# Linear attention and a multiplicative FFN in one kernel: part of the casts and of phi's first instructions on GpSimd, in a new order of steps

## The chip, the core and the metric

The kernel runs on one core of a Trainium2 chip. The metric is the device time of one execution in microseconds (us), lower is better. A profile of one execution shows where that time goes; its span is the time from the first to the last event on the core, a little less than the device time.

## What is computed

```python
def phi(x):
    return np.where(x > 0, x, np.exp(x) - 1.0) + 1.0
# q, k, v: 8 batches, 8 heads, 576 positions, 64 columns, float32
q_p, k_p = phi(q), phi(k)
kv  = einsum('bhsd,bhse->bhde', k_p, v)
num = einsum('bhsd,bhde->bhse', q_p, kv)
den = einsum('bhsd,bhd->bhs', q_p, sum of k_p over s)[..., None] + 1e-06
x   = (num / den), as 4608 tokens by 512 columns
a, b = x @ w1, x @ w2              # w1, w2: 512 x 1024
out = ((a * b) @ w3) @ w_out       # w3: 1024 x 1024, w_out: 1024 x 512; out: 4608 x 512 float32
```

## The kernel before

**Algebra.** The kernel first multiplies w3 by w_out (the product is called Wf, 1024 x 512), so that the FFN is (a * b) @ Wf. All matmuls of the FFN and of Wf take bf16; inputs come from HBM as float32 and are cast.

**Steps and queues.** All work is cut into 490 steps, and the string ORDER lists them. The last lines of the kernel go through ORDER and call one small function per step (s_T3 for T3 and so on). Nothing reorders them afterwards: each engine and each DMA queue works off its instructions in the order of the string, and waits where an operand isn't there or a buffer isn't free. So ORDER sets the order on TensorE (PE), VectorE (DVE), ScalarE (ACT), GpSimd (POOL) and on SyncE's DMA queue (SP), which issues nearly all DMAs. A last letter a, v or p names the engine of a step that can be done by several: ACT, DVE or POOL.

The steps, with the letters of their indices:

- **Loads** (SP, 512 or 576 KB each, into one of 13 buffers): L3.i is block i of w3 (8 blocks; block 0 comes as two halves, LH.0.0 and LH.0.1), LO.x a quarter of w_out, LA.x and LB.x quarters of w1 and w2 (6 and 7 hold columns 0 to 511, 2 and 3 the rest), LQ.b.h, LK.b.h, LV.b.h half of the heads of batch b.
- **Casts**: CO.x, CA.x, CB.x cast such a quarter to bf16 (128 x 1024, lines 207, 211, 216), C3.i a block of w3 (line 227), VC.b.h a half of v (128 x 1152, line 285).
- **Wf**: T3.i.x transposes half of block i of w3 on PE (four 128 x 128 transposes, line 241) and copies the result to SBUF (line 242); FW.i.x does two of the eight matmuls of row block i of Wf (line 253), and needs CO.x; after the last (x = 3) Wf's block is cast to SBUF (line 255).
- **phi**: phi(x) is computed as min(max(x, 0) + 1, exp(x)). PT.n.b.h (n is q or k) does the max and the add in one instruction from float32 to bf16 (line 275, on DVE), EX.n.b.h the exponential on ACT (line 263), and PM.n.b.h the min on DVE (line 282).
- **Attention**: KV and KB build k_p^T v (line 298; KV half a batch in two 64-row tiles, KB a whole batch), QP transposes phi(q) on PE (line 326) and QD does it by DMA instead (line 331); ND (one tile of 128 tokens) and NT with NM (three tiles) form numerator and denominator on PE (line 344) and divide on DVE (line 350). KV, KB, ND and NT use PE in tiles of 64 x 64.
- **x transposed**: XP on PE (line 403, copy on line 404), XD by DMA transpose (line 408).
- **FFN**: chunks c0 of 512 tokens, 9 of them. F.c0.f is block f of 8: four matmuls for a, four for b (line 428, 128 x 512 each), a copied from PSUM by ACT (line 437), and a * b on DVE (line 439). FI does one of the two sides of an F, FP half the tokens of a side, for chunk 0 while the weights arrive. O.t multiplies token tile t by Wf (8 matmuls, line 463) and copies the result out of PSUM (line 470). Q.35 is the last tile, in pieces. S.t stores a tile (two DMAs of 128 KB).

PSUM holds four banks for FFN and Wf ("mm") and two double banks for the rest ("at"). Each F takes two of the four banks, so the second F after one needs its banks again.

**Start.** Nothing of chunk 0 can start before w3, w_out, w1, w2 and batch 0 have passed the DMA queue, 13 loads at a time, so for the first 45 us PE works on what has arrived: w3's transposes and Wf, then batch 0, then chunk 0.

What the change touches is ORDER and s_PT (line 273); copy_of (line 123) already gives GpSimd's copy for the letter p. The prediction's steps are in s_CO, s_CA, s_CB, s_VC, s_EX, s_PM, s_F and s_FI.

Of the kernel before, what the change touches and what calls it, by code (L numbers as in the profile page):

```python
# [18 lines left out]


ORDER = """
L3.2 I.0 LO.0 I.1 T3.2.0.a CO.0.v FW.2.0.a T3.2.1.a LO.1 CO.1.a L3.4 T3.4.0.v T3.4.1.v H.1 L3.3
T3.3.0.a LO.2 FW.4.0.v FW.4.1.a LO.3 L3.5 T3.3.1.v C3.5.a CO.2.v FW.2.1.a FW.2.2.a CO.3.v FW.2.3.v
L3.6 C3.6.v FW.3.0.a FW.3.1.v LK.0.0 T3.5.0.v LH.0.0 T3.5.1.v LQ.0.0 FW.4.2.v EX.k.0.0 PT.k.0.0
FW.4.3.a EX.q.0.0 T3.6.0.v PM.k.0.0 FW.5.0.v FW.5.1.v L3.1 T3.6.1.a PT.q.0.0 PM.q.0.0 L3.7 FW.5.2.v
FW.6.0.a FW.3.2.a FW.3.3.v FW.5.3.v LQ.0.1 T3.1.0.a C3.7.v T3.1.1.a FW.1.0.v FW.1.1.a LK.0.1
PT.q.0.1 EX.q.0.1 PM.q.0.1 T3.7.0.a FW.6.1.v FW.6.2.a FW.6.3.a LV.0.0 I.2 T3.0.0.v LV.0.1 EX.k.0.1
PT.k.0.1 T3.7.1.a LH.0.1 FW.7.0.a FW.7.1.v FW.1.2.v VC.0.0.v QP.0.0.v QP.0.1.a FW.7.2.a KV.0.0.a
PM.k.0.1 VC.0.1.v FW.7.3.v FW.1.3.a KV.0.1.v T3.0.1.a ND.0 FW.0.0.v LA.6 ND.1 FW.0.1.v CA.6.a LA.7
CA.7.a ND.2 FW.0.2.a XP.0.a XP.1.a ND.3 FW.0.3.a FP.0.0.0.0 LB.6 LQ.1.1 EX.q.1.1 LB.7 LA.3 XP.2.v  # L30
XP.3.v FP.0.1.0.0 CB.7.a LA.2 FP.0.1.0.1 LB.3 PT.q.1.1 PM.q.1.1 FI.0.2.0 FI.0.3.0 CB.6.v FI.0.1.1
LB.2 CA.2.a LQ.1.0 CB.3.v FP.0.0.0.1 FI.0.0.1 FI.0.3.1 CB.2.v QP.1.1.v CA.3.a PT.q.1.0 LK.1.0
FI.0.2.1 PT.k.1.0 EX.q.1.0 PM.q.1.0 F.0.4 EX.k.1.0 PM.k.1.0 F.0.5 LV.1.0 VC.1.0.a F.0.6 LK.1.1
EX.k.1.1 PT.k.1.1 PM.k.1.1 LV.1.1 LK.3.0 KV.1.0.a VC.1.1.a F.0.7 LQ.3.1 QP.1.0.a KV.1.1.v PT.k.3.0
EX.q.3.1 EX.k.3.0 O.0.a LQ.3.0 EX.q.3.0 PT.q.3.1 ND.4 ND.5 O.1.a XP.4.a ND.6 ND.7 PM.k.3.0 LK.2.0
XP.5.a O.2.a PM.q.3.1 XP.6.v XP.7.v LQ.2.1 EX.k.2.0 LQ.2.0 PT.k.2.0 PM.k.2.0 PT.q.3.0 EX.q.2.0
LK.3.1 PM.q.3.0 O.3.a LV.4.1 F.1.0 LV.2.0 LK.4.1 S.0.s F.1.1 PT.q.2.1 EX.q.2.1 S.1.s PT.k.3.1 F.1.2
EX.k.3.1 PM.k.3.1 LK.2.1 PM.q.2.1 F.1.3 VC.2.0.a LV.2.1 PT.k.2.1 PT.q.2.0 PM.q.2.0 EX.k.2.1 F.1.4
LV.3.0 F.1.5 VC.2.1.a PM.k.2.1 F.1.6 LV.3.1 VC.3.0.v QD.2.1 EX.k.4.1 KB.2.a QD.2.0 VC.3.1.a ND.8
QD.3.0 F.1.7 KB.3.a NT.9 NM.9.0 NM.9.1 QD.3.1 XD.2.0 NM.9.2 XD.2.1 S.2.s LK.4.0 O.4.v O.5.v NT.12  # L40
LV.4.0 NM.12.0 O.6.v NM.12.1 O.7.v NM.12.2 LQ.4.1 PT.k.4.0 F.2.0 F.2.1 F.2.2 F.2.3 F.2.4 EX.k.4.0
PT.k.4.1 LQ.5.1 F.2.5 PM.k.4.1 F.2.6 VC.4.0.a LQ.4.0 VC.4.1.a PM.k.4.0 F.2.7 S.3.s S.4.s LQ.5.0
LK.5.1 PT.q.5.0 EX.q.5.0 NT.15 PM.q.5.0 EX.q.4.1 NM.15.0 PT.q.4.1 PM.q.4.1 PT.q.4.0 LQ.7.1 S.5.s
KB.4.a PT.k.5.1 O.8.v EX.k.5.1 S.6.s LK.5.0 EX.k.5.0 PT.k.5.0 XD.3.0 XD.3.1 O.9.a O.10.a O.11.v
LV.5.1 F.3.0 PM.k.5.1 LK.6.0 F.3.1 PM.k.5.0 EX.q.4.0 NM.15.1 NM.15.2 LV.5.0 S.7.s S.8.s LK.6.1 F.3.2
S.9.s S.10.s VC.5.0.v PM.q.4.0 QD.4.0 EX.k.6.0 QD.4.1 F.3.3 F.3.4 EX.q.5.1 PT.q.5.1 PM.q.5.1
PT.k.6.1 F.3.5 F.3.6 F.3.7 QD.5.1 O.12.v NT.18 QD.5.0 NM.18.0 XD.4.0 NM.18.1 VC.5.1.a PT.k.6.0
KB.5.a XD.4.1 LQ.6.1 O.13.a O.14.v PT.q.7.1 O.15.v F.4.0 EX.q.7.1 PM.q.7.1 F.4.1 F.4.2 NM.18.2
LK.7.0 F.4.3 NT.21 EX.k.6.1 NM.21.0 NM.21.1 NM.21.2 LV.6.0 VC.6.0.v F.4.4 F.4.5 S.11.s S.12.s
PT.k.7.0 LK.7.1 LQ.7.0 F.4.6 LV.6.1 VC.6.1.v S.13.s S.14.s F.4.7 PT.q.7.0 PM.k.6.1 LQ.6.0 PM.k.6.0  # L50
O.16.v EX.q.7.0 O.17.v PM.q.7.0 PT.q.6.1 LV.7.0 O.18.v XD.5.0 XD.5.1 EX.q.6.1 PM.q.6.1 LV.7.1
VC.7.0.a S.15.s EX.q.6.0 KB.6.a NT.24 O.19.v NM.24.0 PT.q.6.0 PM.q.6.0 QD.6.1 F.5.0 VC.7.1.v
EX.k.7.1 PT.k.7.1 F.5.1 F.5.2 EX.k.7.0 NM.24.1 NM.24.2 QD.7.1 PM.k.7.0 F.5.3 F.5.4 QD.6.0 PM.k.7.1
F.5.5 S.16.s S.17.s NT.27 XD.6.0 NM.27.0 NM.27.1 QD.7.0 KB.7.a NM.27.2 F.5.6 XD.6.1 XD.7.0 F.5.7
S.18.s NT.30 S.19.s O.20.v S.20.s F.6.0 NM.30.0 NM.30.1 NM.30.2 F.6.1 XD.7.1 O.21.v NT.33 O.22.v
NM.33.0 NM.33.1 O.23.v F.6.2 F.6.3 F.6.4 F.6.5 F.6.6 F.6.7 F.7.0 F.7.1 F.7.2 F.7.3 F.7.4 F.7.5 F.7.6
S.21.s S.22.s S.23.s XD.8.0 NM.33.2 XD.8.1 O.24.a O.25.v O.26.v O.27.v S.24.s S.25.s S.26.s S.27.s
F.7.7 F.8.0 F.8.1 F.8.2 F.8.3 F.8.4 F.8.5 F.8.6 F.8.7 O.28.a O.29.a O.30.a S.28.s S.29.s S.30.s
O.31.v S.31.s O.32.v S.32.s O.33.v S.33.s O.34.a S.34.b Q.35
"""  # L60


# [1 line left out]
def kernel(  # L64
# [202 lines left out]
    def by_set(n, t):  # L267

        if n == "k":
            return t.rearrange("p (c j d) -> p c j d", c=2, j=J)  # L270
        return t.rearrange("p (j c d) -> p c j d", c=2, j=J)

    def s_PT(n, b, h, e):
        t = phs[n, b, h] = take("ph" + n, None, [P, HW], BF16, "ph" + n)
        nc.vector.tensor_scalar(out=by_set(n, t), in0=by_set("k", raw[n, b, h]), scalar1=0.0, scalar2=1.0,  # L275
                                op0=ALU.max, op1=ALU.add)
# [254 lines left out]
```

## Time and profile before

| | us |
|---|---|
| median of 3 runs | 243.22 |
| lowest, highest | 242.29, 243.37 |
| the profiled execution | 241.6 |
| its span | 239.8 |
| PE busy in it | 227.6 |
| DVE busy | 157.9 |
| ACT busy | 113.9 |
| POOL busy | 1.3 |

The profile gives, per engine, the busy time and groups of equal instructions with the mean duration of one in nanoseconds; the chain of waits goes back from the last instruction to what released each step. In a row of the timeline the first number is the start and the second the duration, both in us, "x4" counts the instructions merged into the row, and brackets hold the idle time before it and what ended it. PE's matmuls overlap each other, so a row of them is longer than the time that it adds; the chain gives what it adds.

### The profile page before, as it was taken

To read this page: it belongs to the slowest core of one execution; us is meant where nothing else is said; L and a number is where in the kernel's file an instruction comes from. 1 tells how busy PE (TensorE), PEld (TensorE's weight loads), DVE (VectorE), ACT (ScalarE), POOL (GpSimd) and SP (SyncE) were. 2 spreads that over 40 slices of the span, in tenths; PEclk is the share of its full clock that TensorE was granted. 3 is DMA by queue.
4 is the path that set the end of the run, shared out by engine and by line. 5 is a ranking of instruction groups with operands and counts; after the bars stand their busy time and mean duration, and the time that the engine had idled before them with its cause. 6 is when DMAs were issued, how large, how long until landed. Compare 5 with 4: busy or idle time off the path is not lost.

```text
span 239.8 us, 5452 instructions
## 1 busy us (share of the span) xinstructions
PE 227.6 (95%) x2218; PEld 114.4 (48%) x2237; DVE 157.9 (66%) x287; ACT 113.9 (48%) x166; POOL 1.3 (1%) x9
## 2 busy tenths in 40 slices
...
GB/s 247 420 382 403 387 386 389 389 392 389 400 278 129 160 347 392 340 190 358 233 108 271 385 362 177 169 202 112 137 121 78 3 0 44 164 13 0 46 155 148
DMA packets 52041, 55.79 MB, mean 233 GB/s; under 512 B 31281, under 2 KB 31537, under 8 KB 52017
## 3 DMA queue, kind: packets, MB, share of 16 engines
...
q8 instruction: 17, 0.28, 0.5%
q10 hardware_dynamic: 240, 0.26, 0.3%
...
## 4 chain that ended last, share of the span: by engine, by line
PE 92%; DMA 3%; issue 2%; DVE 1%; SPq 1%; ACT 0%; DVEq 0%
PE b_ps L428 26%; PE o_ps L463 26%; PE a_ps L428 26%; PE wf_ps L253 5%; PE nd L344 3%; DMA w<-in_moe_w_dram 3%; PE w3p L241 2%; PE kbp L298 2%; PE qp L326 1%; PE xp L403 1%; PE kvp L298 1%; SPq L155 1%; DVE xt L404 0%; DVE ab L439 0%; DVE w3t L242 0%
## 5 line engine op out<-in xcount | busy, mean ns | idle before, releaser
L428 PEld LDWEIGHTS <-w_sb 128*128 128x128 bf16 x584 | 56.5, 98 | 67.2 <-issue 1.4
L437 ACT COPY a_sb<-a_ps 128x512 f32<-128x512 f32 x72 | 42.2, 587 | 80.4 <-PE a_ps L428 78.5
L439 DVE TENSOR_TENSOR ab<-a_sb,b_ps 128x512 bf16<-128x512 f32 x72 | 49.0, 685 | 38.2 <-PE b_ps L428 36.4
L428 PE MATMUL a_ps<-xt,w_sb 128*128 128x512 bf16 (+1 forms) x296 | 74.0, 373 | 0.1
L428 PE MATMUL b_ps<-xt,w_sb 128*128 128x512 bf16 x288 | 73.8, 379 | 0.1
L463 PE MATMUL o_ps<-wf_sb,ab 128*128 128x512 bf16 (+2 forms) x290 | 63.5, 368 | 1.2 <-issue 0.6
L463 PEld LDWEIGHTS <-ab 128*128 128x128 bf16 x304 | 28.3, 98 | 31.2
L470 DVE COPY o_sb<-o_ps 128x512 f32<-128x512 f32 x23 | 15.8, 689 | 20.7 <-PE o_ps L463 18.9
L350 DVE TENSOR_TENSOR xn<-nd,r 128x512 bf16<-128x512 f32 (+2 forms) x45 | 24.2, 577 | 0.5
L263 ACT ACTIVATE eq<-q 128x1152 bf16<-128x1152 f32 x16 | 18.4, 1164 | 4.8 <-DVE phk L282 3.1
L263 ACT ACTIVATE ek<-k 128x1152 bf16<-128x1152 f32 x16 | 18.7, 1167 | 2.6 <-DMA k<-in_k_dram 2.6
L253 PE MATMUL wf_ps<-wo_sb,w3t 128*128 128x512 bf16 x59 | 16.0, 387 | 2.6 <-DVE wo_sb L207 1.8
L470 ACT COPY o_sb<-o_ps 128x512 f32<-128x512 f32 x12 | 6.9, 581 | 15.0 <-PE o_ps L463 15.0
L275 DVE TENSOR_SCALAR phk<-k 128x1152 bf16<-128x1152 f32 x16 | 12.0, 752 | 1.3 <-DMA k<-in_k_dram 1.3
L282 DVE TENSOR_TENSOR phq<-phq,eq 128x1152 bf16<-128x1152 bf16 x16 | 12.0, 751 | 1.2 <-ACT eq L263 0.5
L241 PE MATMUL w3p<-ident,w 128*128 128x128 f32 x40 | 8.2, 352 | 4.8 <-DMA w<-in_moe_w_dram 4.8
L282 DVE TENSOR_TENSOR phk<-phk,ek 128x1152 bf16<-128x1152 bf16 x16 | 11.9, 751 | 0.2
L275 DVE TENSOR_SCALAR phq<-q 128x1152 bf16<-128x1152 f32 x16 | 12.0, 752 | 0.0
L285 ACT CAST vt<-v 128x1152 bf16<-128x1152 f32 x9 | 10.3, 1160 | 0.0
L241 PEld LDWEIGHTS w3p<-ident,w 128*128 128x128 f32 x40 | 7.0, 214 | 6.4 <-issue 4.7
L253 PEld LDWEIGHTS <-w3t 128*128 128x128 bf16 x64 | 5.6, 98 | 7.1 <-issue 1.5
L344 PEld LDWEIGHTS <-qt 64*64 64x64 bf16 x576 | 6.2, 106 | 4.6 <-issue 3.0
...
## 6 DMA issues: line engine op xcount, KB each, us to landing
k<-in_k_dram SPq DMA_DIRECT2D x16, 576.0 KB, 9.0
q<-in_q_dram SPq DMA_DIRECT2D x16, 576.0 KB, 9.3
v<-in_v_dram SPq DMA_DIRECT2D x16, 576.0 KB, 7.9
...
w<-in_moe_w_dram SPq DMA_DIRECT2D x7, 512.0 KB, 9.5
wo<-in_moe_w_out_dram SPq DMA_DIRECT2D x4, 512.0 KB, 6.7
wa<-in_moe_w_dram SPq DMA_DIRECT2D x4, 512.0 KB, 11.5
wb<-in_moe_w_dram SPq DMA_DIRECT2D x4, 512.0 KB, 11.4
```

Source lines behind the costliest of these rows:

```text
L241: nc.tensor.transpose(tp[:, c, :], blocks[:, 2 * x + c // 2, c % 2, :], idt)
L253: nc.tensor.matmul(wfs[i], w3ts[i][:, c, :], wo_sb[:, c, :], start=(c == 0), stop=(c == FC - 1))
L263: nc.scalar.activation(out=t, in_=raw[n, b, h], func=AF.Exp)
L275: nc.vector.tensor_scalar(out=by_set(n, t), in0=by_set("k", raw[n, b, h]), scalar1=0.0, scalar2=1.0, op0=ALU.max, op1=ALU.add)
L282: nc.vector.tensor_tensor(out=t, in0=t, in1=by_set("k", es[n, b, h]), op=ALU.min)
L344: nc.tensor.matmul(dst[g * R:(g + 1) * R], qts[b, a // 2][rows, j, a % 2 * R:(a % 2 + 1) * R], kvs[b][rows, a // 2, a % 2, :], start=True, ...
L350: nc.vector.tensor_tensor(out=xn[:, :, a0:a1], in0=n4[:, :, :, 0:D], in1=r.unsqueeze(3).to_broadcast([P, 2, a1 - a0, D]), op=ALU.mult)
L428: nc.tensor.matmul(ops_[key][:, tiles.start * P:tiles.stop * P], w[:, w_row(kc), f * P:(f + 1) * P], xts[c0][:, tiles, kc, :], start=(kc = ...
L437: nc.scalar.copy(out=a_sbs[c0, f], in_=ops_[key])
L439: nc.vector.tensor_mul(out=abs_[c0][:, f, :], in0=a_sbs[c0, f], in1=ops_[key])
L463: nc.tensor.matmul(o_ps, abs_[c0][:, f, m * P:(m + 1) * P], wf_sb[:, f, cols], start=(f == 0), stop=(f == FC - 1))
L470: copy_of(e)(out=o_sbs[t], in_=o_ps)
```

## The change

ORDER is a new one, with the same 490 steps. Letters differ: 34 steps carry p, so they run on POOL, which had none but a few small ones before.

| steps | before | after |
|---|---|---|
| PT (32) | 32 DVE | 13 DVE, 19 POOL |
| VC (16) | 9 ACT, 7 DVE | 5 ACT, 4 DVE, 7 POOL |
| CO (4) | 1 ACT, 3 DVE | 1 DVE, 3 POOL |
| CA, CB (8) | 5 ACT, 3 DVE | 2 ACT, 1 DVE, 5 POOL |
| O (35) | 12 ACT, 23 DVE | 25 ACT, 10 DVE |

Smaller moves between ACT and DVE: T3 (9 ACT and 7 DVE before, 6 and 10 after), XP (4 and 4, then 7 and 1), QP (2 and 2, then 4 and 0), KB (6 and 0, then 4 and 2), KV (2 and 2, then 3 and 1). The loads come in another order: q.0.1 is 5th instead of 15th, w_out's second to fourth quarters are 6th to 8th instead of 3rd, 6th and 7th, the halves of w3's block 0 are 18th and 21st instead of 11th and 19th, and q.1.1 is 32nd, behind all weights, instead of 23rd. Which w3 blocks are cast to bf16 first (5, 6, 7), and which transposes run on PE and which by DMA, is as before.

```diff
@@ s_PT
-        nc.vector.tensor_scalar(out=by_set(n, t), in0=by_set("k", raw[n, b, h]), scalar1=0.0, scalar2=1.0,
-                                op0=ALU.max, op1=ALU.add)
+        (nc.gpsimd if e == "p" else nc.vector).tensor_scalar(
+            out=by_set(n, t), in0=by_set("k", raw[n, b, h]), scalar1=0.0, scalar2=1.0,
+            op0=ALU.max, op1=ALU.add)
@@ ORDER, up to the end of chunk 1, and the tail
-L3.2 I.0 LO.0 I.1 T3.2.0.a CO.0.v FW.2.0.a T3.2.1.a LO.1 CO.1.a L3.4 T3.4.0.v T3.4.1.v H.1 L3.3
-T3.3.0.a LO.2 FW.4.0.v FW.4.1.a LO.3 L3.5 T3.3.1.v C3.5.a CO.2.v FW.2.1.a FW.2.2.a CO.3.v FW.2.3.v
-L3.6 C3.6.v FW.3.0.a FW.3.1.v LK.0.0 T3.5.0.v LH.0.0 T3.5.1.v LQ.0.0 FW.4.2.v EX.k.0.0 PT.k.0.0
-FW.4.3.a EX.q.0.0 T3.6.0.v PM.k.0.0 FW.5.0.v FW.5.1.v L3.1 T3.6.1.a PT.q.0.0 PM.q.0.0 L3.7 FW.5.2.v
-FW.6.0.a FW.3.2.a FW.3.3.v FW.5.3.v LQ.0.1 T3.1.0.a C3.7.v T3.1.1.a FW.1.0.v FW.1.1.a LK.0.1
-PT.q.0.1 EX.q.0.1 PM.q.0.1 T3.7.0.a FW.6.1.v FW.6.2.a FW.6.3.a LV.0.0 I.2 T3.0.0.v LV.0.1 EX.k.0.1
-PT.k.0.1 T3.7.1.a LH.0.1 FW.7.0.a FW.7.1.v FW.1.2.v VC.0.0.v QP.0.0.v QP.0.1.a FW.7.2.a KV.0.0.a
-PM.k.0.1 VC.0.1.v FW.7.3.v FW.1.3.a KV.0.1.v T3.0.1.a ND.0 FW.0.0.v LA.6 ND.1 FW.0.1.v CA.6.a LA.7
-CA.7.a ND.2 FW.0.2.a XP.0.a XP.1.a ND.3 FW.0.3.a FP.0.0.0.0 LB.6 LQ.1.1 EX.q.1.1 LB.7 LA.3 XP.2.v
-XP.3.v FP.0.1.0.0 CB.7.a LA.2 FP.0.1.0.1 LB.3 PT.q.1.1 PM.q.1.1 FI.0.2.0 FI.0.3.0 CB.6.v FI.0.1.1
-LB.2 CA.2.a LQ.1.0 CB.3.v FP.0.0.0.1 FI.0.0.1 FI.0.3.1 CB.2.v QP.1.1.v CA.3.a PT.q.1.0 LK.1.0
-FI.0.2.1 PT.k.1.0 EX.q.1.0 PM.q.1.0 F.0.4 EX.k.1.0 PM.k.1.0 F.0.5 LV.1.0 VC.1.0.a F.0.6 LK.1.1
-EX.k.1.1 PT.k.1.1 PM.k.1.1 LV.1.1 LK.3.0 KV.1.0.a VC.1.1.a F.0.7 LQ.3.1 QP.1.0.a KV.1.1.v PT.k.3.0
-EX.q.3.1 EX.k.3.0 O.0.a LQ.3.0 EX.q.3.0 PT.q.3.1 ND.4 ND.5 O.1.a XP.4.a ND.6 ND.7 PM.k.3.0 LK.2.0
-XP.5.a O.2.a PM.q.3.1 XP.6.v XP.7.v LQ.2.1 EX.k.2.0 LQ.2.0 PT.k.2.0 PM.k.2.0 PT.q.3.0 EX.q.2.0
-LK.3.1 PM.q.3.0 O.3.a LV.4.1 F.1.0 LV.2.0 LK.4.1 S.0.s F.1.1 PT.q.2.1 EX.q.2.1 S.1.s PT.k.3.1 F.1.2
-EX.k.3.1 PM.k.3.1 LK.2.1 PM.q.2.1 F.1.3 VC.2.0.a LV.2.1 PT.k.2.1 PT.q.2.0 PM.q.2.0 EX.k.2.1 F.1.4
-LV.3.0 F.1.5 VC.2.1.a PM.k.2.1 F.1.6 LV.3.1 VC.3.0.v QD.2.1 EX.k.4.1 KB.2.a QD.2.0 VC.3.1.a ND.8
-QD.3.0 F.1.7 KB.3.a NT.9 NM.9.0 NM.9.1 QD.3.1 XD.2.0 NM.9.2 XD.2.1 S.2.s LK.4.0 O.4.v O.5.v NT.12
...
-NM.33.0 NM.33.1 O.23.v F.6.2 F.6.3 F.6.4 F.6.5 F.6.6 F.6.7 F.7.0 F.7.1 F.7.2 F.7.3 F.7.4 F.7.5 F.7.6
-S.21.s S.22.s S.23.s XD.8.0 NM.33.2 XD.8.1 O.24.a O.25.v O.26.v O.27.v S.24.s S.25.s S.26.s S.27.s
-F.7.7 F.8.0 F.8.1 F.8.2 F.8.3 F.8.4 F.8.5 F.8.6 F.8.7 O.28.a O.29.a O.30.a S.28.s S.29.s S.30.s
-O.31.v S.31.s O.32.v S.32.s O.33.v S.33.s O.34.a S.34.b Q.35
+L3.1 LO.0 L3.5 I.0 I.1 T3.1.0.v T3.1.1.v C3.5.v T3.5.0.v L3.2 T3.2.0.a LQ.0.1 LO.1 PT.q.0.1.v H.1
+CO.0.p LO.3 FW.5.0.v LO.2 L3.7 FW.2.0.v CO.1.p L3.4 L3.3 T3.5.1.v CO.3.p FW.1.0.a LQ.0.0 PT.q.0.0.p
+EX.q.0.1 PM.q.0.1 I.2 L3.6 LK.0.0 LV.0.0 VC.0.0.p LK.0.1 LV.0.1 LH.0.0 T3.2.1.a CO.2.v LA.7 LA.6
+C3.7.v FW.2.1.a QP.0.1.a LH.0.1 FW.1.1.v FW.1.2.a FW.1.3.a LB.6 LB.7 FW.5.1.v FW.5.2.a CA.6.p LA.2
+EX.q.0.0 FW.5.3.v T3.7.0.v FW.2.2.a FW.2.3.v T3.4.0.v LA.3 FW.7.0.a T3.7.1.v C3.6.a PT.k.0.0.v
+T3.4.1.a T3.3.0.a LQ.1.0 FW.4.0.a FW.4.1.v EX.k.0.0 CB.6.p LB.3 LB.2 FW.7.1.a FW.7.2.a FW.7.3.a
+T3.3.1.v PM.k.0.0 LK.1.0 CB.7.p FW.4.2.v FW.4.3.a T3.6.0.a PM.q.0.0 CA.2.p LK.1.1 FW.3.0.v EX.k.0.1
+T3.6.1.v PT.q.1.0.p FW.3.1.v FW.3.2.v QP.0.0.a CB.2.p KV.0.0.a FW.6.0.a FW.6.1.v FW.6.2.a PT.k.1.0.p
+PT.k.0.1.v PM.k.0.1 LV.1.0 VC.0.1.v KV.0.1.a T3.0.0.a ND.0 FW.3.3.a ND.1 LQ.1.1 CA.7.a FW.0.0.v
+FW.0.1.a ND.2 XP.0.a XP.1.a ND.3 FW.6.3.a T3.0.1.v XP.2.a FP.0.0.0.0 FP.0.1.0.0 XP.3.v FW.0.2.a
+FW.0.3.a FP.0.0.0.1 LV.1.1 FI.0.3.0 FI.0.3.1 EX.q.1.0 FI.0.0.1 PM.q.1.0 LV.2.0 FP.0.1.0.1 FI.0.1.1
+CA.3.a FI.0.2.0 CB.3.v FI.0.2.1 EX.k.1.0 LK.2.1 F.0.4 LK.3.0 QP.1.0.a VC.1.0.v PM.k.1.0 PT.k.1.1.p
+F.0.5 LQ.2.1 EX.k.1.1 PM.k.1.1 PT.q.1.1.p F.0.6 EX.q.1.1 PM.q.1.1 KV.1.0.a VC.1.1.a F.0.7 QP.1.1.a
+KV.1.1.v LQ.3.1 O.0.a LQ.2.0 LK.2.0 ND.4 ND.5 O.1.a XP.4.a PT.q.3.1.p LV.3.0 ND.6 PT.k.2.1.p ND.7
+PT.q.2.0.v EX.k.2.1 LK.3.1 XP.5.a O.2.a PT.k.3.0.p LV.2.1 LQ.4.0 LV.3.1 XP.6.a XP.7.a VC.2.0.p
+LQ.3.0 EX.q.2.0 PT.k.2.0.v PM.k.2.1 EX.k.2.0 PM.k.2.0 O.3.a S.0.s PT.q.2.1.v F.1.0 S.1.s PM.q.2.0
+VC.2.1.p QD.2.0 PT.q.3.0.p F.1.1 EX.k.3.0 PM.k.3.0 F.1.2 PT.k.3.1.p EX.q.3.1 EX.k.3.1 F.1.3 F.1.4
+PM.q.3.1 ND.8 VC.3.0.a EX.q.2.1 KB.2.a EX.q.3.0 PM.q.2.1 QD.2.1 PM.q.3.0 QD.3.0 F.1.5 F.1.6 PM.k.3.1
+F.1.7 QD.3.1 VC.3.1.p KB.3.a NT.9 NM.9.0 NM.9.1 XD.2.0 O.4.a O.5.a NM.9.2 XD.2.1 S.2.s NT.12 NM.12.0
+LK.5.0 LQ.5.0 LK.4.0 S.3.s O.6.a PT.k.4.0.p O.7.a F.2.0 PT.k.5.0.v S.4.s F.2.1 NM.12.1 NM.12.2
...
+PM.q.7.1 NM.27.1 O.20.v O.21.v QD.7.0 O.22.a F.6.0 F.6.1 S.18.s S.19.s S.20.s S.21.s F.6.2 F.6.3
+F.6.4 F.6.5 NM.27.2 S.22.s O.23.a QD.7.1 NT.30 NM.30.0 S.23.s NM.30.1 XD.7.0 NM.30.2 F.6.6 F.6.7
+O.24.v O.25.a O.26.a XD.7.1 F.7.0 F.7.1 F.7.2 O.27.v S.24.s NT.33 NM.33.0 S.25.s S.26.s XD.8.0
+NM.33.1 NM.33.2 F.7.3 F.7.4 F.7.5 XD.8.1 S.27.s F.7.6 F.7.7 F.8.0 F.8.1 F.8.2 O.28.v O.29.a O.30.a
+F.8.3 F.8.4 F.8.5 S.28.s S.29.s S.30.s O.31.a F.8.6 F.8.7 S.31.s O.32.a S.32.s O.33.a S.33.s O.34.a
+S.34.b Q.35
```

28 lines of the change are left out of this document (13 added, 15 removed).

## Prediction

> **What bounds the kernel now.** First the page: the span, each engine's busy share, the chain that ended last, and the sizes of loads.
>
> ```profile
> span 239.8 us, 5452 instructions
> ...
> PE 227.6 (95%) x2218; PEld 114.4 (48%) x2237; DVE 157.9 (66%) x287; ACT 113.9 (48%) x166; POOL 1.3 (1%) x9
> ...
> PE 92%; DMA 3%; issue 2%; DVE 1%; SPq 1%; ACT 0%; DVEq 0%
> ...
> k<-in_k_dram SPq DMA_DIRECT2D x16, 576.0 KB, 9.0
> ...
> wo<-in_moe_w_out_dram SPq DMA_DIRECT2D x4, 512.0 KB, 6.7
> ```
>
> PE is the chain for 92% of the span. Next the list of who waits for whom, the stages (columns: PE, PEld, DVE, ACT, POOL busy, granted clock, DMA share, GB/s), and the chain within the long middle stage.
>
> ```profile
> DVE ab L439 <- PE b_ps L428: 36.4, 42, 1.3
> ```
>
> ```profile
> 14.43:34.66 20.23, 19.36 (x253) 11.64 (x258) 17.14 (x34) 13.79 (x20) 0.00 (x0) 1.00 1.05 390
> 34.66:44.70 10.04, 9.94 (x66) 5.56 (x66) 8.50 (x15) 8.09 (x11) 0.00 (x0) 1.00 1.05 386
> ...
> 60.44:222.80 162.36, 161.41 (x1575) 76.36 (x1585) 110.82 (x199) 70.39 (x108) 0.00 (x0) 1.00 0.74 190
> ```
>
> ```profile
> by line: PE b_ps L428 34.1%; PE a_ps L428 33.8%; PE o_ps L463 25.6%; PE nd L344 2.8%; PE kbp L298 2.5%; issue 0.7%; DVE ab L439 0.4%; DVEq L439 0.0%
> ```
>
> In its commonest instruction DVE waits for PE, 36.4 us in all, not PE for DVE. From 60.44 to 222.80 only issue and DVE are not PE in the chain: 0.7% and 0.4% of 162.36 us, 1.8 us. So relief of DVE or ACT is worth at most that there, whatever its size. From 14.43 to 44.70 the DMA share is 1.05: the loads run without a break, and they set when work becomes possible. What PE loses at the start shows in the chain up to 60 us (start, duration, what):
>
> ```profile
> 2.14 6.33 DMA w<-in_moe_w_dram
> ...
> 12.59 0.48 PE w3p L241 x4
> ...
> 13.09 0.69 DVE w3t L242
> 13.78 0.61 DVE wo_sb L207
> ...
> 17.80 0.22 PE w3p L241 x4
> 18.02 0.86 PE wf_ps L253 x4
> ...
> 20.26 1.56 issue
> 21.81 0.59 ACT w3t L242
> ...
> 31.70 0.25 PE nd L344 x16
> ...
> 35.26 0.24 PE xp L403 x4
> ...
> 35.52 0.85 DVE xt L404 x2
> ...
> 43.13 0.86 PE a_ps L428 x4
> ...
> 50.56 0.50 PE qp L326 x9
> 51.06 0.41 PE kvp L298 x36
> 51.48 0.16 issue
> ```
>
> Four losses: 6.33 us until the second w3 block (PE works for part of that on the first), 1.3 us at 13.09 and 13.78 (w3t, then w_out's cast on DVE), 2.2 us at 20.26 and 21.81, 0.85 us at 35.52 (xt's copies). So at most 1.3 + 2.2 + 0.85 = 4.4 us could be won by an order of the start, if the loads allowed it. The other rows give what a step adds to the chain: a T3 0.48 (0.22 in bf16), an FW 0.43, an ND 0.25, an XP 0.24, half an F 0.86, a QP 0.50, a KV 0.41.
>
> **The change part by part.**
>
> *GpSimd's price.* POOL's trace ends after 2 us with these rows; the durations on the other engines stand beside them.
>
> ```profile
> L138 POOL CAST ident<-ident 128x128 bf16<-128x128 f32 x1 | 0.3, 289 | 0.1
> masks.py:197 POOL MEMSET ident<- 128x128 f32 x1 | 0.2, 204 | 0.3 <-POOLq L515 0.3
> L515 POOL MEMSET const-bfloat16-1.0<- 128x1 bf16 x1 | 0.1, 101 | 0.0
> ```
>
> ```profile
> L439 DVE TENSOR_TENSOR ab<-a_sb,b_ps 128x512 bf16<-128x512 f32 x72 | 49.0, 685 | 38.2 <-PE b_ps L428 36.4 <-ACT a_sb L437 1.5
> ...
> L263 ACT ACTIVATE eq<-q 128x1152 bf16<-128x1152 f32 x16 | 18.4, 1164 | 4.8 <-DVE phk L282 3.1 <-DMA q<-in_q_dram 1.7
> ...
> L275 DVE TENSOR_SCALAR phq<-q 128x1152 bf16<-128x1152 f32 x16 | 12.0, 752 | 0.0
> ...
> L282 DVE TENSOR_TENSOR phq<-phq,eq 128x1152 bf16<-128x1152 bf16 x16 | 12.0, 751 | 1.2 <-ACT eq L263 0.5
> ...
> L285 ACT CAST vt<-v 128x1152 bf16<-128x1152 f32 x9 | 10.3, 1160 | 0.0
> ...
> L285 DVE CAST vt<-v 128x1152 bf16<-128x1152 f32 x7 | 5.3, 756 | 0.0
> ...
> L207 DVE CAST wo_sb<-wo 128x1024 bf16<-128x1024 f32 x3 | 2.0, 687 | 4.3 <-DMA wo<-in_moe_w_out_dram 4.3
> ```
>
> A cast of 128 columns takes 289 ns, a memset of one column 101: (289 - 101) / 127 = 1.48 ns a column, so an estimate of 1.61 us for 1024 columns and 1.80 us for 1152. I take these, since the cast is the only row that reads and converts as the new ones do. Low end, by the memset of 128 columns: (204 - 101) / 127 = 0.81 ns, 0.93 and 1.04 us. High end, the cast's row without a fixed part: 8 x 0.289 = 2.31 and 9 x 0.289 = 2.60 us. DVE does the same in 0.69 and 0.75 us, ACT a v in 1.16. The Trainium skill, GPSIMD Engine Reference, § Performance versus the Vector engine, speaks against the move: for elementwise work it calls GpSimd structurally slower, but gives 1.03 to 1.8 cycles an element at 1.2 GHz for light loops, 0.99 to 1.73 us for 1152; by that the sum would be at its better end.
>
> *Load on the engines.* POOL gets 8 x 1.61 + 26 x 1.80 = 59.7 us (34.5 to 86.1), DVE loses 19 x 0.752 = 14.3 us for PT alone. None of it is on PE's chain: worth 0 by itself. What counts is when each result is there, below.
>
> *The start.* The loads are the clock of this stage. Two rows fix their pace:
>
> ```profile
> 4.24 1.10 PE L241 MATMUL w3p<-ident,w 128*128 128x128 f32 x4 [4.24 <-DMA w<-in_moe_w_dram]
> ...
> 31.63 0.21 PEld L344 LDWEIGHTS <-qt 64*64 64x64 bf16 x16 [0.42 <-issue]
> ```
>
> ```profile
> 43.23 1.16 ACT L263 ACTIVATE eq<-q 128x1152 bf16<-128x1152 f32 x1 [1.49 <-DMA q<-in_q_dram]
> ```
>
> The first 512 KB are there at 4.24; q.1.0, the 29th load, at 43.23, after 19 units of 512 KB (halves joined) and 8 of 576: 14,336 KB in 38.99 us, 1.39 us per 512 KB and 1.57 per 576. By this pace the new order has w_out's 2nd quarter at 11.4, its 4th at 12.8 and 3rd at 14.2, v.0.1 at 27.6, LB.7 at 34.5, LB.2 at 41.7, k.1.0 at 43.2, q.1.1 at 47.9, v.1.1 at 49.5. In PE's order:
>
> - CO.1 on POOL is done at 11.4 + 1.61 = 13.0, so FW.2.1 starts there; CO.2 stays on DVE: 14.2 + 0.69 = 14.9, FW.1.2 ends at 15.4 (CO.3 on POOL, 14.6, is in time).
> - From there to F.0.4 PE has 26 FW (11.2 us), 6 T3 in float32 (2.9) and 4 in bf16 (0.9), QP.0.0, 2 KV (1.3), 4 ND (1.0), 4 XP (1.0), 4 FP at 0.43 (1.7) and 6 FI (5.2): 25.2 us, 40.6 without a wait. I add 1.3 us for three waits: KV.0.1 for v.0.1 and its cast (28.4), ND's two banks, T3.0.1 and x's copies behind them. F.0.4 begins at 41.9.
> - Before, F.0.4 is the row at 43.13, with QP.1.1 (0.50) already done: like for like 42.6. So 0.7 us are won so far.
> - F.0.4's b side, at 41.9 + 0.86 = 42.8, needs CB.2 on POOL: 41.7 + 1.61 = 43.3. The win shrinks by 0.5 us; F.0.4 ends at 44.2.
> - QP.1.0, F.0.5 to F.0.7 and KV.1.0 take 6.1 us, to 50.3. QP.1.1 needs q.1.1 through PT on POOL and PM: 47.9 + 1.80 + 0.75 = 50.5. KV.1.1 ends at 51.4; before, the chain passes that point at 51.48.
>
> So the start is worth -0.1, call it 0. With POOL's low prices CB.2 and PT.q.1.1 come in time and it is -0.9; with the high ones +0.7.
>
> *PM behind POOL.* DVE works in order: where a PM waits for its PT on POOL, the a * b of the F's behind it (685 ns) waits too, and PE stops when an F's bank isn't free for the second F after it. Worst is q.3.0, the last load of its group, 13 loads after v.1.1: 49.5 + 13 x 1.57 = 69.9. F.1.0 at 60.44 as before, five F (8.65), ND.8 and KB.2 (0.25 and, as an estimate, two KV, 0.82) put F.1.5 at 70.2, the end of its matmuls at 71.9 and of its product at 72.6. PT is done at 71.7 and PM at 72.5, so the product ends at 73.1. F.1.7's b needs that bank at 70.2 + 2 x 1.73 + 0.86 = 74.5. Cover 1.4 us, cost 0; with 2.60 us for PT the product ends at 73.9, still 0. Buffers of loads that POOL frees later: 13 of them, and a load is issued some 9 us ahead (page's last column) of the 18 us that 13 loads take, so 0.
>
> *64 x 64 groups.* PE turns to 64 x 64 tiles 21 times instead of 20; the timeline's row at 31.63 shows 0.42 us of idle weight loading at such a turn. +0.3 (0 to 0.42).
>
> *The end.* F.8.7 now stands directly ahead of O.32, whose first seven matmuls (7 x 0.216) cover its product; the last tile is stored as before: 0. O on ACT instead of DVE: both wait for PE: 0.
>
> **Sum:** 0 + 0.3 on the profiled execution, 241.6 (span 239.8 and 1.8 around it), gives 241.9. That execution lies 1.6 below the median of 243.22, so the prediction for the median is 243.5, with 242.3 to 244.4 from the bounds above. A measurement of this kernel tells about 0.5% (1.2 us) from no change.
>
> **The rivals.**
>
> 1. *The start wins.* The three waits don't happen, POOL costs its low price and the loads keep up: F.0.4 at 40.6 against 42.6, minus 2.0; some of the 1.8 us of the middle stage may go too. With the 0.3 for the turns: 241.5, at best 239.7. It needs LB.2 at 40.5 or so instead of 41.7, a pace of 1.35 us per 512 KB. For it: 4.4 us of losses in the chain. Against: LB.2 is the 28th load in both orders, and the DMA share is 1.05.
> 2. *POOL and DVE hold each other up* while both work from SBUF: a PM, PT or cast on DVE waits until a running POOL instruction ends. At the start PM.q.0.1 (due 11.4: q.0.1 at 10.0, EX of 1.16 us behind a copy on ACT) stands behind CO.1 to 13.0, then CO.3 behind PM, CO.2 behind CO.3: FW.1.2 comes at 16.1 instead of 15.0, +1.1. Later, 29 POOL instructions (51 us) lie between LA.6's landing (31.1) and the middle of chunk 5 (60.44, four chunks and their O at 12 x 1.73, half a chunk: some 150), four tenths of the time. So of some 40 PM and PT on DVE there 16 wait half a POOL instruction, 0.9 us, 14 us in all. Where delays add up beyond the cover of 1.4 us PE stops; with a fifth felt, +3. Sum 243.2 + 1.1 + 3 + 0.3 = 247.6. It decides from the point where one wait and the instruction's own 0.75 us outlast the cover. No row bears on it, as POOL is idle after 2 us. The Trainium skill, SBUF — State Buffer, § Who interferes with whom, says this: DVE in a 2-port mode, or with two SBUF inputs, and GpSimd lock each other out of a shared port pair for a whole instruction; by it, this rival's time.
> 3. *POOL's two-operation PT is dearer* than any row bounds, say 4 us: CB.2's place is kept, but PT.q.1.1 is done at 51.9 and QP.1.1 waits to 52.7: +2.2; and F.1.5's product ends at 75.3, 0.8 late: in sum 243.2 + 2.2 + 0.8 + 0.3 = 246.5. POOL's load would be 117 us, still no bound.
>
> **How the numbers follow.** Forecast 0.38; the start wins 0.26; hold-up 0.22; dear PT 0.14. Range 240.8 to 247.6: it reaches to the rivals on both sides and leaves out a start that wins more and a hold-up felt more. Faster by over 0.5%: rival 1 and a little of the forecast's low end, 0.28. Slower by over 0.5%: rivals 2 and 3, 0.36. Within: 0.36.
>
> **What would show it.** POOL casts of 1.6 and PT of 1.8 us; KV.1.1's end near 51.4; no PE gap from F.1.5 to F.1.7; 21 turns to 64 x 64. DVE's PM and PT longer than 0.75 us, or gaps ahead of them while POOL runs, speak for rival 2; PE waiting for w_out's or w2's casts by POOL breaks the step on the start. I am wrong above all if the pace of the loads differs in the new order.

## The result and the profile after

The changed kernel takes **275.15 us** (median of 4 runs, 272.97 to 275.89) against 243.3 us of the kernel before beside it (4 runs): a ratio of **1.130** (95% interval 1.1225 to 1.138), 32 us slower. The forecast of 243.5 us and its range are far below that, and so is each rival's time. The profiled execution took 275.85 us. (Some executions of a kernel fall in a slower state; in what follows medians are over all runs and ratios over the undisturbed ones, so that a ratio of medians can differ from the ratio given by up to 1.5%.)

The page of the kernel after: span, busy time of the engines, granted clock of PE in 40 slices (tenths; a slice is 6.85 us), and the chain that ended last by engine.

```profile
span 274.1 us, 5490 instructions
...
PE 236.8 (86%) x2237; PEld 116.3 (42%) x2237; DVE 169.0 (62%) x247; ACT 116.8 (43%) x172; POOL 99.7 (36%) x43
...
PEclk9999998685899999999999999998899999999999
...
PE 60%; DMA 14%; DVE 13%; POOL 4%; issue 4%; ACT 2%; SPq 1%; DVEq 0%; ACTq 0%
```

PE has fallen from 92% of the chain to 60%; DMA, DVE and POOL are in it with 14, 13 and 4%. Of DMA's part, 29.7 us are four loads ahead of 40 us, which came nearly as early as foreseen (below), and 9.9 us two transposes of phi(q) by DMA (at 93.69 and 156.78) that PE waits for. Though 40 instructions fewer run on DVE (247 instead of 287), it is busy for 11.1 us more than the 157.9 of before. PE is busy for longer with the same matmuls, 236.8 us instead of 227.6; but before's trace lacks 19 of the 2237 matmul records, and the last kernel of experiment 6, which has them all, shows 230.0, so some 7 us are real. PE's clock is clearly below full speed from the 7th to the 11th slice, 41 to 75 us. The groups on POOL, and the ones on DVE that answer to them:

```profile
L276 POOL TENSOR_SCALAR phq<-q 128x1152 bf16<-128x1152 f32 x11 | 46.5, 4229 | 17.2 <-DMA q<-in_q_dram 17.2
L276 POOL TENSOR_SCALAR phk<-k 128x1152 bf16<-128x1152 f32 x8 | 34.5, 4322 | 38.8 <-DMA k<-in_k_dram 38.8
L287 POOL CAST vt<-v 128x1152 bf16<-128x1152 f32 x7 | 9.0, 1306 | 15.3 <-DMA v<-in_v_dram 15.3
...
L217 POOL CAST w_sb<-wb 128x1024 bf16<-128x1024 f32 x3 | 3.1, 1041 | 1.3 <-DMA wb<-in_moe_w_dram 1.3
```

```profile
L441 DVE TENSOR_TENSOR ab<-a_sb,b_ps 128x512 bf16<-128x512 f32 x72 | 49.0, 684 | 61.3 <-PE b_ps L430 59.8 <-ACT a_sb L439 1.4
L284 DVE TENSOR_TENSOR phk<-phk,ek 128x1152 bf16<-128x1152 bf16 x16 | 23.8, 1492 | 0.1
L284 DVE TENSOR_TENSOR phq<-phq,eq 128x1152 bf16<-128x1152 bf16 x16 | 23.4, 1462 | 3.1 <-POOL phq L276 2.8 <-ACT eq L264 0.2
...
L276 DVE TENSOR_SCALAR phk<-k 128x1152 bf16<-128x1152 f32 x8 | 14.3, 1792 | 2.1 <-DMA k<-in_k_dram 2.1
...
L276 DVE TENSOR_SCALAR phq<-q 128x1152 bf16<-128x1152 f32 x5 | 5.4, 1084 | 1.0 <-DMA q<-in_q_dram 1.0
```

Two things are new. A PT takes 4.2 to 4.3 us on POOL, against 0.752 on DVE, while v's cast, of the same size, takes 1.31 and that of a quarter of w2 1.04. And the same PM and PT on DVE take 1.1 to 1.8 us each instead of 0.75, while the product a * b, which reads one of its inputs from PSUM, keeps its 684 ns. DVE's idle time before a PM that was ended by a PT on POOL is 2.8 us in all: DVE hardly waits for POOL's *results*. Its instructions themselves grow long.

The timeline from 38 to 58 us shows it at single instructions (start, duration, what; brackets: idle time before and what ended it):

```profile
39.65 4.09 POOL L276 TENSOR_SCALAR phq<-q 128x1152 bf16<-128x1152 f32 x1 [1.80 <-DMA q<-in_q_dram]
...
43.70 1.04 POOL L217 CAST w_sb<-wb 128x1024 bf16<-128x1024 f32 x1
43.78 1.57 DVE L284 TENSOR_TENSOR phq<-phq,eq 128x1152 bf16<-128x1152 bf16 x1 [2.81 <-POOL phq L276]
44.70 9.09 POOL L276 TENSOR_SCALAR phk<-k 128x1152 bf16<-128x1152 f32 x2
...
45.88 3.98 DVE L217 CAST w_sb<-wb 128x1024 bf16<-128x1024 f32 x1
...
49.91 1.46 PE L430 MATMUL b_ps<-xt,w_sb 128*128 128x512 bf16 x3 [3.53 <-DVE w_sb L217]
...
54.33 4.28 DVE L284 TENSOR_TENSOR phk<-phk,ek 128x1152 bf16<-128x1152 bf16 x1
```

At 43.78 a PM starts just after a POOL cast and takes 1.57 us. At 45.88 CB.3, a cast on DVE, starts in the middle of POOL's PT.k.1.0 (44.70) and takes 3.98 us; PE's matmuls of F.0.4 wait 3.53 us for it. At 54.33 a PM beside the next PT takes 4.28 us. What PE loses by that, in five stretches of 10 us (columns: PE, PEld, DVE, ACT, POOL busy with counts, granted clock, DMA share, GB/s), and the chain behind it:

```profile
30.00:40.00 10.00, 10.00 (x130) 6.12 (x125) 5.49 (x15) 6.69 (x12) 4.52 (x5) 1.00 1.03 376
40.00:50.00 10.00, 4.61 (x24) 2.05 (x22) 7.09 (x6) 4.48 (x6) 10.00 (x4) 0.82 1.05 394
50.00:60.00 10.00, 7.65 (x69) 3.75 (x70) 8.96 (x6) 5.21 (x7) 10.00 (x3) 0.84 1.05 391
60.00:70.00 10.00, 4.61 (x53) 2.23 (x52) 7.93 (x5) 2.14 (x3) 10.00 (x3) 0.51 0.78 289
70.00:80.00 10.00, 10.00 (x118) 5.21 (x117) 7.69 (x14) 6.77 (x11) 10.00 (x5) 0.98 0.25 54
```

```profile
45.95 3.91 DVE w_sb L217
...
59.21 2.56 DVE phk L284
...
63.43 3.63 DVE phq L284
...
68.88 2.58 PE o_ps L465 x8
...
78.56 0.86 PE a_ps L430 x4
```

POOL is busy without a break from 40 to 80 us. In each of the three stretches from 40 to 70 us DVE gets 5 or 6 instructions done, and PE works for 16.9 of the 30 us. There PE is granted 0.51 to 0.84 of its clock, as a mean over each stretch: the eight matmuls of O.0 at 68.88 take 2.58 us, where those of an O take 8 x 0.216 = 1.73. (The Trainium skill, TensorE: Matmul & The Clock Gate, § What's actually happening, states such a gate, half the clock after an idle window; the trace agrees, with 0.50 from 64.00 to 68.88.) Before, O.0 and F.1.0 stand in the chain as

```profile
51.63 1.67 PE o_ps L463 x7
...
60.44 0.87 PE a_ps L428 x4
```

F.1.0 starts at 78.56 instead of 60.44, so 18.1 of the 34.3 us by which the span grew are lost by then.

### The profile page after: what moved, and what is told of

Its sections match the earlier page's. It is cut to its first block, busy times and chain, and to the rows that moved or that the text cites. A ratio compares the mean times of both kernels' runs of the same rounds, so it can differ in the third digit from the quotient of the medians.

```text
span 274.1 us, 5490 instructions
## 1 busy us (share of the span) xinstructions
PE 236.8 (86%) x2237; PEld 116.3 (42%) x2237; DVE 169.0 (62%) x247; ACT 116.8 (43%) x172; POOL 99.7 (36%) x43
## 4 chain that ended last, share of the span: by engine, by line
PE 60%; DMA 14%; DVE 13%; POOL 4%; issue 4%; ACT 2%; SPq 1%; DVEq 0%; ACTq 0%
PE o_ps L465 20%; PE b_ps L430 19%; PE a_ps L430 18%; DMA q<-in_q_dram 6%; DMA qt<-phq 4%; DVE phq L284 3%; POOL phq L276 3%; DVE phk L284 3%; DVE ab L441 3%; DMA w<-in_moe_w_dram 2%; DMA wa<-in_moe_w_dram 2%; DVE phk L276 1%; DVE w_sb L217 1%; PE nd L346 1%; PE qp L328 1%
## 5 line engine op out<-in xcount | busy, mean ns | idle before, releaser
L465 PE MATMUL o_ps<-wf_sb,ab 128*128 128x512 bf16 (+2 forms) x304 | 66.8, 371 | 2.6 <-DVE ab L441 1.5
L276 POOL TENSOR_SCALAR phq<-q 128x1152 bf16<-128x1152 f32 x11 | 46.5, 4229 | 17.2 <-DMA q<-in_q_dram 17.2
L276 POOL TENSOR_SCALAR phk<-k 128x1152 bf16<-128x1152 f32 x8 | 34.5, 4322 | 38.8 <-DMA k<-in_k_dram 38.8
L472 ACT COPY o_sb<-o_ps 128x512 f32<-128x512 f32 x25 | 14.7, 587 | 48.0 <-PE o_ps L465 45.6
L284 DVE TENSOR_TENSOR phq<-phq,eq 128x1152 bf16<-128x1152 bf16 x16 | 23.4, 1462 | 3.1 <-POOL phq L276 2.8
L284 DVE TENSOR_TENSOR phk<-phk,ek 128x1152 bf16<-128x1152 bf16 x16 | 23.8, 1492 | 0.1
L276 DVE TENSOR_SCALAR phk<-k 128x1152 bf16<-128x1152 f32 x8 | 14.3, 1792 | 2.1 <-DMA k<-in_k_dram 2.1
L287 POOL CAST vt<-v 128x1152 bf16<-128x1152 f32 x7 | 9.0, 1306 | 15.3 <-DMA v<-in_v_dram 15.3
L329 ACT COPY qt<-qp 128x1152 bf16<-128x1152 bf16 x4 | 4.5, 1119 | 15.3 <-PE qp L328 15.3
L346 PE MATMUL nd<-kv,qt 64*64 64x65 bf16 x576 | 8.2, 194 | 2.2 <-DMA qt<-phq 2.2
L472 DVE COPY o_sb<-o_ps 128x512 f32<-128x512 f32 x10 | 6.8, 686 | 5.3 <-PE o_ps L465 5.3
```

Of the source, the lines that this page charges most:

```text
L276: (nc.gpsimd if e == "p" else nc.vector).tensor_scalar(out=by_set(n, t), in0=by_set("k", raw[n, b, h]), scalar1=0.0, scalar2=1.0, op0=ALU. ...
L284: nc.vector.tensor_tensor(out=t, in0=t, in1=by_set("k", es[n, b, h]), op=ALU.min)
L287: copy_of(e)(out=vts[b % 2][:, h, :, :, 0:D], in_=raw["v", b, h].rearrange("p (c j d) -> p c j d", c=2, j=J))
L346: nc.tensor.matmul(dst[g * R:(g + 1) * R], qts[b, a // 2][rows, j, a % 2 * R:(a % 2 + 1) * R], kvs[b][rows, a // 2, a % 2, :], start=True, ...
L465: nc.tensor.matmul(o_ps, abs_[c0][:, f, m * P:(m + 1) * P], wf_sb[:, f, cols], start=(f == 0), stop=(f == FC - 1))
L472: copy_of(e)(out=o_sbs[t], in_=o_ps)
```

## The experiments

**My theory after the result:** POOL's PT of 4 us is the cause, because POOL and DVE hold each other up while both work from SBUF. **Rivals:** the new order is bad by itself, wherever the 34 steps run; POOL's results come too late, without any hold-up; the casts do it.

**1. POOL and DVE by themselves.** The kernel before, with a bench after its last step: first POOL alone, then POOL beside DVE. Its time isn't compared with anything.

```diff
+        g.tensor_copy(out=Y, in_=X)
+        g.tensor_scalar(out=Y, in0=X, scalar1=0.0, scalar2=1.0, op0=ALU.max, op1=ALU.add)
+        g.tensor_scalar_max(out=Y, in0=X, scalar1=0.0)
...
+        g.tensor_scalar(out=Y, in0=A, scalar1=0.0, scalar2=1.0, op0=ALU.max, op1=ALU.add)
...
+                    v.tensor_tensor(out=C, in0=C, in1=A, op=ALU.min)
...
+                    v.tensor_scalar(out=G, in0=W, scalar1=0.0, scalar2=1.0, op0=ALU.max, op1=ALU.add)
...
+                    v.tensor_copy(out=G[:, 0:NCH], in_=pt)
```

X and W are float32, Y, A, C and G are bf16, pt is a PSUM bank. These lines are 507, 508, 509, 512, 519 (PM's kind), 521 (PT's kind, on DVE) and 523 (from PSUM) of that kernel; line 528 is POOL's PT again, beside DVE's.

> The kernel before with a bench behind its last step: POOL instructions alone (a cast, PT's two operations, one operation of it, from float32 and bf16), then a POOL instruction (PT, two casts, memsets) beside four DVE instructions of one kind (PM's, PT's, a copy from PSUM). Theory: PT on POOL takes 4.1 us also alone, a cast 1.1 to 1.2; one operation less takes clearly less; beside POOL's PT the first DVE instruction of PM's or PT's kind waits for POOL's end, about 4 us, and a copy from PSUM takes its 0.4 to 0.7 us untouched; beside memsets, which read nothing, PM's kind isn't held up. Rival: POOL's PT takes about 1.8 us alone and is stretched to 4.1 by DVE; or DVE is slowed by a constant share, each instruction by the same factor.

Measured (timeline; "x3" are three instructions in one row):

```profile
239.04 1.15 POOL L507 CAST my<-mx 128x1152 bf16<-128x1152 f32 x1 [237.02 <-DVE mx L502]
...
240.27 4.09 POOL L508 TENSOR_SCALAR my<-mx 128x1152 bf16<-128x1152 f32 x1
...
244.44 3.12 POOL L509 TENSOR_SCALAR my<-mx 128x1152 bf16<-128x1152 f32 x1
...
254.83 4.09 POOL L512 TENSOR_SCALAR my<-ma 128x1152 bf16<-128x1152 bf16 x1
...
264.75 1.54 DVE L519 TENSOR_TENSOR mc<-mc,ma 128x1152 bf16<-128x1152 bf16 x2
...
267.93 4.47 POOL L528 TENSOR_SCALAR my<-mx 128x1152 bf16<-128x1152 f32 x1 [4.60 <-DVE mx L526]
268.48 5.77 DVE L519 TENSOR_TENSOR mc<-mc,ma 128x1152 bf16<-128x1152 bf16 x3
...
275.02 6.11 DVE L521 TENSOR_SCALAR mg<-mw 128x1152 bf16<-128x1152 f32 x3
...
281.17 2.87 DVE L523 CAST mg<-mp 128x512 bf16<-128x512 f32 x4
281.37 4.09 POOL L528 TENSOR_SCALAR my<-mx 128x1152 bf16<-128x1152 f32 x1 [2.43 <-DVE mx L526]
...
286.35 3.99 DVE L519 TENSOR_TENSOR mc<-mc,ma 128x1152 bf16<-128x1152 bf16 x3
```

Alone, POOL's cast takes 1.15 us, PT 4.09, with one operation 3.12, and bf16 input doesn't help (4.09 at 254.83). So the 4.2 to 4.3 in the kernel are nearly all POOL's own time. Beside a PT, three of PM's kind on DVE take 5.77 us, where three alone take 3 x 0.77 = 2.31: one of them waits some 3.5 us for what is left of POOL's instruction. Three of PT's kind on DVE (275.02) are held in the same way, 6.11 us. Beside two POOL casts (286.35) three of PM's kind take 3.99. Copies from PSUM beside a PT (281.17) are not held, nor is the PT beside them (4.09). Beside three memsets on POOL, which only write, three of PM's kind take 2.34 us and aren't held, while three of PT's kind take 4.95 and are; that second half I hadn't foreseen. The Trainium skill, SBUF — State Buffer, § Who interferes with whom, gives this rule: the two engines share a port pair, and whoever has it keeps it for a whole instruction, if DVE is in a 2-port mode (casts and tensor_scalar between SBUF tiles can be) or has two inputs in SBUF while POOL reads SBUF; a DVE instruction with at most one SBUF input outside these modes goes free. All these rows agree.

**2. Undo parts of the change in place.** Three kernels with after's order and some letters back: the 19 PT on DVE; the 15 casts back on ACT and DVE; all 34.

```diff
-T3.6.1.v PT.q.1.0.p FW.3.1.v FW.3.2.v QP.0.0.a CB.2.p KV.0.0.a FW.6.0.a FW.6.1.v FW.6.2.a PT.k.1.0.p
+T3.6.1.v PT.q.1.0.v FW.3.1.v FW.3.2.v QP.0.0.a CB.2.p KV.0.0.a FW.6.0.a FW.6.1.v FW.6.2.a PT.k.1.0.v
...
-T3.6.1.v PT.q.1.0.p FW.3.1.v FW.3.2.v QP.0.0.a CB.2.p KV.0.0.a FW.6.0.a FW.6.1.v FW.6.2.a PT.k.1.0.p
+T3.6.1.v PT.q.1.0.p FW.3.1.v FW.3.2.v QP.0.0.a CB.2.v KV.0.0.a FW.6.0.a FW.6.1.v FW.6.2.a PT.k.1.0.p
```

The first pair of lines is of the first kernel, the second pair of the second; the third has both edits, and each goes on in the same way through the rest of ORDER.

> The changed kernel with its 19 PT back on DVE; the 15 casts stay on POOL, the order is the new one. Theory: the loss comes from PT on POOL (4.2 us each) and from DVE being held up while they run, so 240 to 247 us, and PM back at about 0.75 us. Rival, the order: if the new order of steps and loads loses the time, above 262. Rival, the casts: if the casts on POOL come late, above 255.

> The changed kernel with its 15 casts of weights and v back on the engines that had them before; the 19 PT stay on POOL. Theory (PT on POOL): 268 to 277 us, close to the changed kernel. Rival, the casts: 243 to 255. Rival, the order: 262 to 277 as well, so this run alone doesn't part the order from PT; with the run that moves PT back it does.

> The new order with nothing on POOL: all 34 steps on the engines that had them before. Theory: the order by itself is worth within 2% of before, 240 to 248 us. Rival, the order: above 262.

Measured: 274.42 us with the PT on DVE (ratio 1.128, 1.122 to 1.134), 294.16 with the casts back (1.206, 1.197 to 1.215), 276.79 with all back (1.134, 1.125 to 1.143). All three lie above the ranges that I expected of my theory. With the casts back on DVE they are held by POOL's PT as well (the three casts of w2 on DVE take 2.22 us each). So taking the casts off POOL doesn't help, but as an edit of the same sort as the other two this run alone doesn't clear them; experiments 5 and 6 do. The first and the third kernel speak against my theory as they stand: with no PT on POOL the loss is still there. The third one's timeline shows what they tested:

```profile
43.20 1.43 DVE L276 TENSOR_SCALAR phk<-k 128x1152 bf16<-128x1152 f32 x2 [0.81 <-DMA k<-in_k_dram]
...
46.22 0.71 PE L300 MATMUL kvp<-vt,phk 64*64 64x65 bf16 x36 [5.23 <-DVE vt L287]
```

PT.k.1.0 stands early in the new order, as is right for an engine that does nothing else. On DVE, which works in order, it stands ahead of PT.k.0.1 and VC.0.1 and waits there for a load that isn't due before 43.2; both are held behind it, and PE waits 5.23 us for v's cast. In the first kernel the same wait of PE is 7.40 us. That is another fault, made by the edit; that such faults make up the whole of these two losses isn't shown. So these two runs can't tell the new order from their own fault, and I moved the PT instead.

**3. The PT on DVE where they are due.** After's order, but each of the 19 PT on DVE directly ahead of its EX (three of them ahead of PM); the casts stay on POOL.

```diff
-T3.6.1.v PT.q.1.0.p FW.3.1.v FW.3.2.v QP.0.0.a CB.2.p KV.0.0.a FW.6.0.a FW.6.1.v FW.6.2.a PT.k.1.0.p
...
-FW.0.3.a FP.0.0.0.1 LV.1.1 FI.0.3.0 FI.0.3.1 EX.q.1.0 FI.0.0.1 PM.q.1.0 LV.2.0 FP.0.1.0.1 FI.0.1.1
+FP.0.0.0.1 LV.1.1 FI.0.3.0 FI.0.3.1 PT.q.1.0.v EX.q.1.0 FI.0.0.1 PM.q.1.0 LV.2.0 FP.0.1.0.1 FI.0.1.1
```

> The changed kernel with its 19 PT on DVE again, each placed directly ahead of its EX (three ahead of their PM) instead of where POOL had it, so that DVE doesn't stand waiting for a load that only POOL could afford to wait for; the 15 casts stay on POOL. Theory: the loss is PT on POOL, 4.09 us each and DVE held up beside it, so 240 to 248 us. Rival, the order: if its loads, whose buffers are given back late (the 20th load waits for v.0.0's cast), cost the time by themselves, above 258.

Measured: 250.77 us (ratio 1.032, 1.027 to 1.036). That is 2.8 us above the range that I expected, but 24 of the 32 us are gone with nothing but the PT taken off POOL and moved. Of the 7.5 us left a part is again a matter of placing, as the chain shows:

```profile
8.36 10.67 DMA q<-in_q_dram
...
53.18 1.04 DVE phq L276
...
56.22 1.83 PE o_ps L465 x8
```

DVE waits for q.0.0's landing until 19.05 with other work behind it, and the PT of q.1.1 comes up on DVE only at 53.1, behind other work and not behind its load (ACT starts the exponential of the same q.1.1 at 51.69), so O.0 starts at 56.22 instead of 51.63. The order, the casts on POOL and my placing together cost these 3%; this run doesn't part them.

**4. POOL's PT as pure extra work.** A PT that nobody reads, on a scratch tile, on POOL: 19 of them in the kernel of experiment 3 where after has its own, and 19 in before's order. All real PT stay on DVE. A copy of one column ahead of each makes it wait for the load.

```diff
+    g.tensor_copy(out=spare[:, 0:1], in_=raw[n, b, h][:, 0:1])
+    g.tensor_scalar(out=spare, in0=spare, scalar1=0.0, scalar2=1.0, op0=ALU.max, op1=ALU.add)
```

> As the run before, but POOL also runs a spare PT (same instruction, on a bf16 scratch buffer, read by nobody) where the changed kernel had its 19. So POOL and DVE meet as in the changed kernel and no result comes late from POOL. Theory, hold-up first: most of the loss of the changed kernel is back, 260 to 285 us. Rival, lateness of PT's result first: 242 to 252.

> The order and the engines of before; beside each of the 19 PT that the change moved, POOL runs a spare one on a scratch buffer that nobody reads. Theory, hold-up: each spare PT (4.1 us) holds one DVE instruction up for up to 4 us, DVE's waits grow by 30 to 70 us, and 255 to 285 us come out. Rival, lateness alone matters: 242 to 248.

Measured: 293.6 us in the new order (ratio 1.191, 1.184 to 1.198, against 1.032 without the spare ones) and 296.83 in before's order (1.2205, 1.213 to 1.2285). Both are above the 285 us that I had expected at most. Nobody reads a spare PT, so no result of it can be late. Two ways remain by which POOL can still be late: in the new order its 15 casts stand behind the spare PT (but in that trace no wait of PE, DVE or ACT ends with POOL), and the one-column copy keeps a load's buffer until POOL comes to it. From the groups of the second kernel:

```profile
L283 POOL TENSOR_SCALAR spare<-spare 128x1152 bf16<-128x1152 bf16 x19 | 80.1, 4215 | 1.6
```

```profile
L279 DVE TENSOR_SCALAR phk<-k 128x1152 bf16<-128x1152 f32 x16 | 31.4, 1960 | 1.2 <-DMA k<-in_k_dram 1.2
L289 DVE TENSOR_TENSOR phk<-phk,ek 128x1152 bf16<-128x1152 bf16 x16 | 21.8, 1367 | 0.2
```

80.1 us of POOL's work make DVE busy for 207.7 us instead of 157.9, 49.8 more, and the kernel 53 us slower. One stretch of its chain goes through a spare PT and a load of q behind it (114.70 to 126.56), so up to 12 of the 53 us may be a late load. The 41 that are left are still more than the whole loss of the change: the hold-up alone is enough for it. (That it costs more here than in the change may come of the 19 more instructions on DVE that can be held; that is argued.)

**5. The size of POOL's instruction.** After's order and engines, with POOL's 19 PT made shorter: as a plain cast (its max and add are left out of these 19) or with the max alone (the add is left out).

```diff
+            nc.gpsimd.tensor_copy(out=by_set(n, t), in_=by_set("k", raw[n, b, h]))
...
+            nc.gpsimd.tensor_scalar_max(out=by_set(n, t), in0=by_set("k", raw[n, b, h]), scalar1=0.0)
```

The first line is the one version, the second the other, each for the letter p alone.

> The changed kernel, order and engines untouched, but POOL's 19 PT are plain casts to bf16 (the max and the add are left out of these), so each takes about 1.15 us instead of 4.09. Theory, the length of PT on POOL is the cause: 243 to 252 us, below the run with PT on DVE if its own placing cost something. Rival, the order of steps and loads: above 258.

> The changed kernel, but POOL's 19 PT do only the max (the add is left out of these): 3.12 us instead of 4.09. Theory, loss grows with the length: in a straight line between a cast's 1.15 us (about 248) and 275 at 4.09 it would be 266; 258 to 270. Rival, a threshold at the cover of 1.4 us that I forecast: beyond it nearly every us counts on the path, so the same 266 or less; rival, lateness doesn't matter: 272 to 278.

Measured: 246.34 us (ratio 1.011, 1.007 to 1.015) and 263.54 us (1.085, 1.080 to 1.090). The groups of the cast version, then of the version with max:

```profile
L277 POOL CAST phq<-q 128x1152 bf16<-128x1152 f32 x11 | 12.6, 1146 | 37.2 <-DMA q<-in_q_dram 28.4 <-DVE r L363 8.8
```

```profile
L286 DVE TENSOR_TENSOR phk<-phk,ek 128x1152 bf16<-128x1152 bf16 x16 | 14.9, 937 | 0.1
```

```profile
L277 POOL TENSOR_SCALAR phq<-q 128x1152 bf16<-128x1152 f32 x11 | 36.5, 3317 | 22.7 <-DMA q<-in_q_dram 19.0 <-PE qp L330 3.7
```

```profile
L286 DVE TENSOR_TENSOR phk<-phk,ek 128x1152 bf16<-128x1152 bf16 x16 | 21.5, 1348 | 0.4 <-ACT ek L264 0.4
```

The order and the engine of every step are the same in these two and in after; only POOL's 19 instructions differ:

| 19 instructions on POOL | q's, ns each | k's PM on DVE, ns | DVE busy, us | profiled execution, us | median, us |
|---|---|---|---|---|---|
| cast | 1146 | 937 | 139.0 | 248.65 | 246.34 |
| max | 3317 | 1348 | 158.6 | 263.59 | 263.54 |
| max and add (after) | 4229 | 1492 | 169.0 | 275.85 | 275.15 |

DVE runs the same 247 instructions in all three, so its busy time grows only by being held: 30.0 us from the cast to the full PT, and the execution grows by 27.2 (by the medians 28.8). About nine tenths of what holds DVE reach the end, though DVE is busy for only 62% of the span; from the cast to the max it is 14.9 of 19.6 us (by the medians 17.2). POOL's results come later in the longer versions too, so a part of this can be lateness. The cast version is also the better bound on the new order: with casts and all, it costs about 1% (1.5% at most by the interval).

**6. The casts alone, in before's order.** First the same 15 casts on POOL, then only CO.2 and CO.3, the casts of w_out at which before's chain has DVE at 13.78.

```diff
-T3.3.0.a LO.2 FW.4.0.v FW.4.1.a LO.3 L3.5 T3.3.1.v C3.5.a CO.2.v FW.2.1.a FW.2.2.a CO.3.v FW.2.3.v
+T3.3.0.a LO.2 FW.4.0.v FW.4.1.a LO.3 L3.5 T3.3.1.v C3.5.a CO.2.p FW.2.1.a FW.2.2.a CO.3.p FW.2.3.v
```

> The order of before, with the same 15 casts (CO, CA, CB, VC) on POOL and all PT on DVE. Theory: POOL casts take 1.04 to 1.3 us, as ACT does, so 240 to 248 us. Rival, the casts: above 252.

> The order of before with only CO.2 and CO.3 on POOL, where the chain of before stood for 0.61 us on a cast of w_out that DVE began late behind a copy. POOL casts take 1.04 us and can start when the load lands. Theory: 0.3 to 1.2 us faster than before, 242 to 243.3. Rival: the loads set the end of the start anyway, so within 0.3%.

Measured: 245.33 us with 15 casts (ratio 1.006, 1.002 to 1.010) and **241.66 us** with two (0.995, 0.9926 to 0.9975), the fastest kernel of this study. The second one's groups and chain:

```profile
L207 POOL CAST wo_sb<-wo 128x1024 bf16<-128x1024 f32 x2 | 2.1, 1040 | 10.3 <-DMA wo<-in_moe_w_out_dram 10.3
```

```profile
14.15 0.47 PE w3p L241 x4
14.62 2.16 PE wf_ps L253 x10
```

Where before's chain goes through DVE for 0.69 and 0.61 us, these two PE pieces follow each other; PE doesn't wait there for a cast. A profiled execution doesn't show the gain of 1.2 us (its first loads landed 0.7 us later, and its span is 240.2); the 12 runs do. That the gain is these 1.3 us of DVE is argued, not shown. Casts of 1.04 us cost little on POOL, and at a point where DVE is late two of them gain.

## Why the prediction was wrong

- **GpSimd's price: the step that failed first.** The casts were priced at 1.61 and 1.80 us with 0.93 and 1.04 as the low end; undisturbed they take 1.04 and 1.15, near that end. But PT was put at the same 1.80, "since the cast is the only row that reads and converts as the new ones do", with 2.60 as the most. It takes 4.09. The bound came from rows of one kind of instruction and was used for another: a cast isn't the nearest row to a tensor_scalar with two operations, and before's trace had none on POOL. The range should have had no such upper end. The estimate from the Trainium skill's rate for light loops (GPSIMD Engine Reference, § Performance versus the Vector engine), 0.99 to 1.73 us, holds for the cast with its 1.15, and not for PT.
- **The hold-up of DVE by POOL has no term in the forecast's sum; it is most of the loss.** It was rival 2, at 0.22, so the mechanism was named and its size failed. It stands in the rows of experiment 1, and experiment 4 shows that it is enough. Its own sum, 16 waits of half a POOL instruction, gave 14 us with an instruction of 1.8; with 4.1 us the same 16 waits give 16 x 2.05 = 33 us. Measured on PM and PT in after: 47.2 + 19.7 = 66.9 us for 45 instructions that take 33.8 at 0.751 each, 33 us of holding. That the two agree so well is partly luck, since with longer instructions POOL also works for a larger part of the time, so that more than 16 should have waited. What failed besides the duration is "with a fifth felt": about nine tenths were (experiment 5). The cover of 1.4 us is shorter than one wait of up to 4 us, so a full wait outlasts it, and PE comes back with a lower clock.
- **Rival 3, the dear PT, had the right price and the wrong effect.** It took 4 us, near what was measured, and gave 246.5 by the lateness of single results. Its load of POOL, 117 us, also puts the 7 casts of v at 4 us; with 1.80 for them it is 101.5, and POOL was busy for 99.7. The two rivals were priced apart, the hold-up with a short PT and the dear PT without hold-up. Each makes the other worse.
- **"Load on the engines": worth 0 failed in the sign.** Taking 14.3 us of PT from DVE put 38 us of holding on it: experiment 3, with all PT on DVE, has it busy for 145.6 us, so 131.3 would be left without the 19, and after has 169.0.
- **The start.** The pace of the loads held: q.1.0 landed at 39.6, by the pace 38.9. POOL's casts of w_out were done at 12.8 and 14.6, as foreseen (13.0, 14.6), the second by luck: it took 1.61 us, as priced, where the one before it took 1.04. CB.2 was done at 44.74 instead of 43.3, as it stood behind PT.q.1.0. The step breaks at CB.3, on DVE, which I took as free: held for 3.98 us, it gives F.0.4 its b side at 49.9.
- **"PM behind POOL" and "buffers of loads", both 0.** Neither is quite nothing. DVE's idle time before PM for POOL's results is 2.8 us, and the chain has POOL's PT twice, for 4.1 us each at 19.66 and 39.65; behind the first, v's cast gives its buffer back only at 25.71, where the chain goes on with a load of w1. But q.1.0 landed just 0.7 us behind the pace, so lateness looks small beside the 38 us of holding. I didn't run it by itself, so its share is argued from the traces alone.
- **The new order** was put at 0.3 us. The cast version puts it at about 1% with all casts on POOL; how much of that is order and how much is held DVE (its PM take 0.94 us) stays open, as do the 3% of experiment 3.
